# Batch 4's loads issued one chunk earlier, and the order of the first two chunks, in a linear-attention and GELU-MLP kernel

## The chip, the cores and the metric

The kernel runs on one core of a Trainium2 chip. The metric is the device time of one execution in microseconds (us), as the median of several runs. Engines are named as in the profile: PE multiplies matrices, DVE and ACT evict and cast and compute exponentials and GELU, POOL does some elementwise work, and SP issues nearly all DMAs.

## What is computed

Two parts, one after the other. Eight batches of eight heads, 576 positions and 64 channels; then a two-layer MLP over the 4608 resulting rows of 512 channels.

```
q_s = softmax(q, axis=-1)          # over a head's 64 channels
k_s = softmax(k, axis=2)           # over the 576 positions
kv  = einsum('bhsd,bhse->bhde', k_s, v)
att = einsum('bhsd,bhde->bhse', q_s, kv)
x   = att.transpose(0, 2, 1, 3).reshape(4608, 512)
h   = x @ w_in                     # w_in  512 x 2048
out = gelu(h) @ w_out              # exact GELU, w_out 2048 x 512
```

Inputs and output are float32. The kernel multiplies in bfloat16.

## The kernel before

**Chunks.** The rows of the MLP are worked on in nine chunks of 512. Chunk c, for c from 0 to 7, is the first 512 positions of batch c; chunk 8 gathers the last 64 positions of all eight batches. A chunk has two phases. `h_phase` makes h transposed, 16 column tiles t of 128x512, each from four matmuls over the row blocks `dm` of w_in (L295), and applies GELU on ACT into the tile g (L300). `y_phase` makes the output, four tiles j, each from 16 matmuls over t (L305); `y_out` evicts a tile with DVE into one of four `y_sb` buffers (L312) and writes it with a DMA on SP (L315).

**What a chunk needs from attention.** Batch b's q is exponentiated on ACT (`exp_q`, L133), its row sums are made on DVE and it is scaled on POOL or DVE (`norm_q`, L196 to L198). It is transposed to `qT`, for batches 0 and 1 on PE (`tp_mm`, L212, evicted by `tp_evac`) and after that by a DMA transpose on SP (`xbar_step`, L231). k is exponentiated (`exp_k`, L138). v is cast to bfloat16 beside a column of ones (`cast_v`, L145). `kv_mm` (L166) multiplies the two, heads in two halves, `kv_norm` (L176, L177) divides by the sums and gives `kvc`. `x_mm` (L251) multiplies qT by kvc, and `x_evac` (L275 on DVE, L277 on ACT) leaves the chunk's x transposed in `xT`.

**Order.** The schedule is written by hand: every engine executes its instructions in the order in which the program states them. `ins` and `yi` hang pieces of later batches' attention behind chosen matmuls: the entry `(j, t)` runs behind the matmul of output tile j and row t. From chunk 2 on, batch c+2 is loaded in the h phase of chunk c, exponentiated before the y phase of c, and its v is cast behind (0, 8) of that y phase; batch c+1's `x_all` stands behind (2, 12). Chunks 0 and 1 are written out, since w_in and w_out arrive during them.

**DMAs.** SP's queue takes loads, DMA transposes and output writes in program order, and a DMA on it waits for what frees its buffer. Loads of q, k and v use two buffers each (`f32in`), so batch 4 takes batch 2's. Weights arrive in float32 in five staging buffers and are cast to bfloat16 by `cast_wi` (L375 on POOL, L379 on DVE) and `cast_wo` (L398). w_in comes in five column groups; group 2 (columns of t=4 to 7) in four parts by dm, groups 3 and 4 in two parts each, cast in as many pieces as they are loaded. w_out comes in four groups of four rows t; the last one, t=12 to 15, in two halves.

**PSUM.** Eight banks: `psum_h` has three one-bank tiles, `psum_y` two, and `psum_a` one single bank ("a") and one pair ("a2"). h tiles rotate through `psum_h`, output tiles through `psum_y`. In chunk 0 all four output tiles are open at once (`yps`, two in `psum_h` and two in `psum_y`) and t is the outer loop, so that w_out can be used as it arrives.

**The order around the change, before.** After row t=11 of chunk 0's outputs, batch 1's two transposes follow, half 0 in "a" and half 1 in `psum_h`; then rows 12 and 13; the first half of batch 1's kv; rows 14 and 15 for tiles 0 and 1 (`y_end`); the first half of x; the second half of kv; rows 14 and 15 for tiles 2 and 3; the second half of x. Batch 4 is loaded in `front3`, which stands behind t=0 of chunk 2's h phase and first normalises q of batch 3 and transposes it:

```
    def front3():
        norm_q(3, 0, 2)
        norm_q(3, 1, 2, nc.vector)
        xbar_step(3)
        load(4)
```

Of the kernel before, what the change touches and what calls it, by code (L numbers as in the profile page):

```python
# [8 lines left out]
FP32 = mybir.dt.float32  # L9
# [7 lines left out]
def kernel(  # L17
# [74 lines left out]
    def load_pair(b, name, t, parts=1):  # L92
        f = f32in.tile([128, HP, NS * D], FP32, tag=name + "f")
        st[b][name + "f"] = f
        src = t[b].rearrange("h (p n) d -> (h p) (n d)", n=NS).rearrange("(x q) f -> q x f", q=128)
        n = HP // parts
        for i in range(parts):
            nc.sync.dma_start(out=f[:, i * n:(i + 1) * n, :], in_=src[:, i * n:(i + 1) * n, :])

    def load(b):  # L100
        load_main(b, "q", q)
        load_pair(b, "k", k)
        load_pair(b, "v", v)
# [40 lines left out]
    def cast_v(b, hp, eng=nc.vector):  # L144
        eng.tensor_copy(  # L145
            out=v_aug[b % 2][:, hp, :, 0:D],
            in_=st[b]["vf"][:, hp, :].rearrange("p (n d) -> p n d", n=NS),
        )
# [5 lines left out]
    def kv_mm(b, half):  # L154


        if "kv" not in st[b]:
            st[b]["kv"] = psum_a.tile([128, 2, 2, 256], FP32, tag="a2", name="kv")
        ps = st[b]["kv"]
        for n in range(NS):  # L160
            for i in range(2):
                for hh in range(2):
                    hp = 2 * half + i
                    pr = slice(hh * 64, hh * 64 + 64)
                    c = slice((hh ^ i) * 64, (hh ^ i) * 64 + 64)
                    nc.tensor.matmul(  # L166
                        ps[c, i, half, 0:D + 1], ek[b % 2][pr, hp, n, :],
                        v_aug[b % 2][pr, hp, n, 0:D + 1], start=(n == 0), stop=(n == NS - 1),
                    )

    def kv_norm(b, h0, h1):

        ps = st[b]["kv"]
        m = h1 - h0
        rec = small.tile([128, 2, 2], FP32, tag="reck")
        nc.vector.reciprocal(rec[:, :, 0:m], ps[:, :, h0:h1, D])  # L176
        nc.vector.tensor_tensor(  # L177
            out=kvc[b].rearrange("p (h i) d -> p i h d", i=2)[:, :, h0:h1],
            in0=ps[:, :, h0:h1, 0:D],
            in1=rec[:, :, 0:m].unsqueeze(3).to_broadcast([128, 2, m, D]), op=ALU.mult,  # L180
        )
# [21 lines left out]
    def tp_mm(b, half):  # L203
        if half == 0:
            st[b]["qT"] = attn_sb.tile([128, J, HP, 128], BF16, tag="qT", name="qT")
        pool, tag = (psum_h, "h") if half == 1 else (psum_a, "a")
        ps = pool.tile([128, J, 2, 128], BF16, tag=tag)
        st[b][f"tp{half}"] = ps
        for i in range(2):
            hp = 2 * half + i  # L210
            for j in range(J):
                nc.tensor.transpose(  # L212
                    ps[:, j, i, :],
                    st[b]["eq"][:, j, 2 * hp:2 * hp + 2, :].rearrange("p h d -> p (h d)"),
                    identity,
                )
# [19 lines left out]
    def x_tile(b, hp, pool, tag):  # L236
        if "xT" not in st[b]:
            st[b]["xT"] = attn_sb.tile([128, HP, M], BF16, tag="xT", name="xT")
        st[b][f"x{hp}"] = pool.tile([128, M], FP32, tag=tag, name="ps")
# [32 lines left out]
    def x_evac(b, hp, eng="v"):  # L272
        ps = st[b][f"x{hp}"]
        if eng == "v":
            nc.vector.tensor_copy(out=st[b]["xT"][:, hp, :], in_=ps)  # L275
        else:
            nc.scalar.copy(out=st[b]["xT"][:, hp, :], in_=ps)  # L277

    def h_phase(c, ins, groups={}, pre={}):


        g = moe_sb.tile([128, NDF, M], BF16, tag="g", bufs=1)
        st[c]["g"] = g
        xT = st[c]["xT"]
        t1 = 0
        while t1 < NDF:
            t0, t1 = t1, t1 + groups.get(t1, 1)
            ts = range(t0, t1)
            pss = [psum_h.tile([128, M], FP32, tag="h", name="ps") for t in ts]
            for dm in range(NDM):  # L290
                if t0 == 0:
                    for f in pre.get(dm, []):
                        f()
                for ps, t in zip(pss, ts):
                    nc.tensor.matmul(  # L295
                        ps, wi_bf[:, dm, t * 128:(t + 1) * 128], xT[:, dm, :],
                        start=(dm == 0), stop=(dm == NDM - 1),
                    )
            for ps, t in zip(pss, ts):
                nc.scalar.activation(out=g[:, t, :], in_=ps, func=AF.Gelu)  # L300
                for f in ins.get(t, []):
                    f()

    def y_mm(c, ps, j, t):
        nc.tensor.matmul(  # L305
            ps, st[c]["g"][:, t, j * 128:(j + 1) * 128], wo_bf[:, t, :],
            start=(t == 0), stop=(t == NDF - 1),
        )

    def y_out(c, ps, j):  # L310
        y_sb = moe_sb.tile([128, DM], FP32, tag="y_sb")
        nc.vector.tensor_copy(out=y_sb, in_=ps)  # L312
        if c < B:
            dst = out[c * S:c * S + M, :].rearrange("(p j) n -> p j n", j=J)[:, j, :]
            nc.sync.dma_start(out=dst, in_=y_sb)  # L315
        else:
            for b2 in range(2):
                r0 = (2 * j + b2) * S + M
                nc.sync.dma_start(out=out[r0:r0 + R, :], in_=y_sb[b2 * R:(b2 + 1) * R, :])
# [48 lines left out]
    def cast_wi(i, w, eng):  # L368
        n = wi_cols[i]
        r = n // 128  # L370
        o = wi_bf[:, :, wi_off[i]:wi_off[i] + n].rearrange("p d (c m) -> p d c m", c=r)
        w = w[:, :, 0:n].rearrange("p d (m c) -> p d c m", c=r)
        if eng == "p":
            for h in range(2):
                nc.gpsimd.tensor_copy(out=o[:, 2 * h:2 * h + 2], in_=w[:, 2 * h:2 * h + 2])  # L375
        else:
            d = NDM // wi_parts[i]
            for c in range(0, NDM, d):
                nc.vector.tensor_copy(out=o[:, c:c + d], in_=w[:, c:c + d])  # L379

    def load_wo(i, parts=1):
        w = wst.tile([128, 4, DM], FP32, tag="w")
        src = moe_w_out[i * 512:(i + 1) * 512, :]
        if i == 0:
            for h in range(2):
                nc.sync.dma_start(
                    out=w[:, 2 * h:2 * h + 2],
                    in_=src[256 * h:256 * h + 256].rearrange("(p c) f -> p c f", c=2),
                )
            return w  # L390
        src = src.rearrange("(p c) f -> p c f", c=4)
        n = 4 // parts
        for h in range(parts):
            nc.sync.dma_start(out=w[:, h * n:(h + 1) * n], in_=src[:, h * n:(h + 1) * n])
        return w

    def cast_wo(i, w, c0=0, n=4):
        nc.vector.tensor_copy(  # L398
            out=wo_bf[:, 4 * i + c0:4 * i + c0 + n, :], in_=w[:, c0:c0 + n]
        )  # L400

    def warm(n, z=zeros):
        ps = psum_y.tile([128, DM], FP32, tag="y")
# [26 lines left out]
    wo = [load_wo(i) for i in range(3)]  # L430
    load_main(1, "q", q, 2)
    load_pair(1, "k", k, 2)
    wo.append(load_wo(3, 2))
    load_pair(1, "v", v, 4)
    load(2)
    nc.vector.memset(zeros32, 0.0)  # L436
    nc.vector.memset(zeros, 0.0)
# [20 lines left out]
    for hp, pool, tag in ((0, psum_y, "y"), (1, psum_y, "y"), (2, psum_a, "a"), (3, psum_h, "h")):  # L458
# [16 lines left out]
        6: [lambda: cast_wi(4, wi[4], "v")],  # L475
        9: [lambda: cast_wo(0, wo[0])],
        12: [lambda: cast_wo(1, wo[1])],
    }, groups={0: 2})


    exp_q(1, parts=2)
# [5 lines left out]
    norm_q(1, 0, 2)  # L487
    norm_q(1, 1, 2, nc.vector)
    cast_wo(3, wo[3], 0, 2)
    cast_wo(3, wo[3], 2, 2)  # L490
    for hp in range(3):
        cast_v(1, hp, nc.gpsimd)
    for t in range(12):
        for j in range(J):
            y_mm(0, yps[j], j, t)
    tp_step(1, 0)
    tp_step(1, 1)
    cast_v(1, 3)
    load(3)
    for t in (12, 13):  # L500
        for j in range(J):
            y_mm(0, yps[j], j, t)

    def y_end(j):
        for t in (14, 15):
            y_mm(0, yps[j], j, t)

    kv_mm(1, 0)
    kv_norm(1, 0, 1)
    y_end(0)  # L510
    y_end(1)
    y_out(0, yps[0], 0)
    x_tile(1, 0, psum_a, "a")
    x_tile(1, 1, psum_h, "h")
    x_mm(1, 0)
    kv_mm(1, 1)
    x_evac(1, 0, "s")
    x_evac(1, 1, "s")
    kv_norm(1, 1, 2)
    y_out(0, yps[1], 1)  # L520
    y_end(2)
    y_end(3)
    xx = psum_a.tile([128, 2, M], FP32, tag="a2", name="xx")
    st[1]["x2"], st[1]["x3"] = xx[:, 0], xx[:, 1]
    x_mm(1, 1)
    x_evac(1, 2)
    x_evac(1, 3, "s")
    y_out(0, yps[2], 2)
    y_out(0, yps[3], 3)
    h_phase(1, {12: [lambda: cast_v_all(2)]}, groups={0: 2})  # L530
# [9 lines left out]
        (1, 1): [lambda: norm_q(2, 1, 2, nc.vector)],  # L540
        (1, 12): [lambda: kv_step(2)],
        (1, 15): [lambda: xbar_step(2)],
        (2, 2): [lambda: cast_v_all(3)],
        (3, 5): [lambda: x_all(2), lambda: kv_step(3)],
    })

# [2 lines left out]
    def front3():  # L549
        norm_q(3, 0, 2)  # L550
        norm_q(3, 1, 2, nc.vector)
        xbar_step(3)
        load(4)

    for c in range(2, B + 1):
        nb = c + 2
# [54 lines left out]
```

The softmax here doesn't subtract the row's maximum and nothing guards it: scores larger than these inputs give would overflow.

## Time and profile before

| | |
|---|---|
| median of 8 runs | 284.03 us (283.29 to 284.47) |
| the profiled execution | 284.47 us |
| its span in the trace | 282.7 us; 1.8 us lie around it |
| granted PE clock | 1.00 |
| PE, ACT, DVE, POOL busy | 95%, 55%, 36%, 12% of the span |
| DMA | 50.10 MB, mean 177 GB/s |

The span is the time from the first to the last instruction of the program in the trace. Times in the timeline and the chain of waits count from its start. A matmul's shown duration (mean 379 ns for the large ones) overlaps the next one's, so spacing is read from starts. An engine's idle time counts only where PE waits for that engine.

### The profile page before, as it was taken

How to read it: one execution, taken by the hardware profiler on the slowest of the kernel's cores; microseconds unless marked ns; L12 is line 12 of the kernel's file. 1: busy time of each engine (PE TensorE's matmuls, PEld its weight loads, DVE VectorE, ACT ScalarE, POOL GpSimd, SP SyncE). 2: the span in 40 equal slices, each digit the busy share in tenths (PEclk: the TensorE clock that was granted, in tenths of full speed). 3: DMA queues.
4: the chain of work that ended last, by engine and by line, in shares of the span. 5: the costliest groups of instructions: out<-in, count | busy, mean ns of one | idle time of the engine just before them, and what ended most of it. 6: DMA issues, size and time to landing. Idle time of an engine off the chain costs nothing.

```text
span 282.7 us, 4527 instructions
## 1 busy us (share of the span) xinstructions
PE 269.8 (95%) x1894; PEld 125.6 (44%) x1922; DVE 102.2 (36%) x150; ACT 156.7 (55%) x242; POOL 32.8 (12%) x25
## 2 busy tenths in 40 slices
PE   7789999999999899999999999999999999999993
PEld 3334454444444344444444444444444444444442
DVE  3767486309760570075006510552016200220021
ACT  5756763789467915693469436853683363136300
POOL 0530041002020050005000500050005000000000
PEclk9999999999999999999999999999999999999999
DMA  7999999951439429911991189127501500210033
GB/s 243 394 381 430 399 400 406 403 217 57 135 84 347 162 97 242 368 41 39 234 378 50 47 206 358 67 77 178 121 0 74 148 2 0 77 74 0 0 77 75
DMA packets 44852, 50.10 MB, mean 177 GB/s; under 512 B 20384, under 2 KB 29856, under 8 KB 44576
## 3 DMA queue, kind: packets, MB, share of 16 engines
q1 hardware_dynamic: 44544, 49.68, 51.6%
q8 instruction: 15, 0.25, 0.4%
q10 hardware_dynamic: 288, 0.13, 0.2%
q14 instruction: 5, 0.04, 0.0%
HBM read 36.70 MB, written 9.44 MB: 163 GB/s over the span
## 4 chain that ended last, share of the span: by engine, by line
PE 72%; DMA 18%; DVE 4%; ACT 2%; issue 1%; SPq 1%; ACTq 0%
PE ps L295 34%; PE ps L305 33%; DMA f<-in_v_dram 9%; DMA f<-in_q_dram 4%; DMA w<-in_moe_w_in_dram 3%; PE kv L166 2%; DMA touch<-in_moe_w_in_dram 2%; PE ps L251 1%; PE ps L327 1%; DVE v_aug L145 1%; DVE qsum L196 1%; ACT ek L138 1%; ACT e L133 1%; DVE e L198 1%; SPq L231 0%
## 5 line engine op out<-in xcount | busy, mean ns | idle before, releaser
L295 PE MATMUL ps<-xT,wi_bf 128*128 128x512 bf16 x565 | 125.7, 379 | 1.6 <-DVE wi_bf L379 1.0
L305 PE MATMUL ps<-wo_bf,g 128*128 128x512 bf16 x543 | 122.3, 379 | 2.7 <-issue 1.1
L300 ACT ACTIVATE g<-ps 128x512 bf16<-128x512 f32 x144 | 85.6, 597 | 68.7 <-PE ps L295 68.7
L295 PEld LDWEIGHTS <-wi_bf 128*128 128x128 bf16 x576 | 56.1, 98 | 69.6 <-DVE wi_bf L379 1.8
L305 PEld LDWEIGHTS <-g 128*128 128x128 bf16 x560 | 53.9, 98 | 65.5 <-issue 1.8
L312 DVE COPY y_sb<-ps 128x512 f32<-128x512 f32 x35 | 23.8, 683 | 75.3 <-PE ps L305 72.3
L198 POOL TENSOR_TENSOR e<-e,recq 128x2048 bf16<-128x2048 bf16 (+1 forms) x9 | 25.7, 2855 | 179.0 <-DVE recq L197 147.0
L145 DVE CAST v_aug<-f 128x576 bf16<-128x576 f32 x26 | 17.9, 745 | 57.1 <-DMA f<-in_v_dram 57.1
L277 ACT CAST xT<-ps 128x512 bf16<-128x512 f32 x19 | 10.2, 588 | 31.6 <-PE ps L251 22.0
L196 DVE TENSOR_REDUCE qsum<-e 128x16 f32<-128x1024 bf16 (+1 forms) x13 | 21.0, 1614 | 14.5 <-ACT e L133 14.5
L133 ACT ACTIVATE e<-f 128x512 bf16<-128x512 f32 (+1 forms) x42 | 20.5, 556 | 2.0 <-DMA f<-in_q_dram 1.7
L138 ACT ACTIVATE ek<-f 128x2304 bf16<-128x2304 f32 (+1 forms) x10 | 17.2, 1730 | 1.7 <-DMA f<-in_k_dram 1.7
L275 DVE CAST xT<-ps 128x512 bf16<-128x512 f32 x15 | 9.7, 685 | 15.4 <-PE ps L251 12.6
L79 ACT ACT_TABLE_LOAD x9 | 11.5, 1283 | 2.8 <-issue 2.6
L405 PE MATMUL ps<-zeros 128*128 128x512 f32 (+1 forms) x14 | 8.0, 716 | 1.5 <-DVE zeros L436 1.5
L133 ACT ACT_TABLE_LOAD x7 | 9.0, 1283 | 0.1
L379 DVE CAST wi_bf<-w 128x512 bf16<-128x512 f32 (+1 forms) x8 | 7.3, 914 | 2.8 <-DMA w<-in_moe_w_in_dram 2.8
L166 PEld LDWEIGHTS <-ek 64*64 64x64 bf16 x576 | 6.5, 105 | 2.9 <-issue 1.1
L166 PE MATMUL kv<-v_aug,ek 64*64 64x65 bf16 x576 | 7.2, 193 | 0.1
L398 DVE CAST wo_bf<-w 128x2048 bf16<-128x2048 f32 (+1 forms) x5 | 5.1, 1014 | 4.8 <-DMA w<-in_moe_w_out_dram 4.8
L198 DVE TENSOR_TENSOR e<-e,recq 128x1024 bf16<-128x1024 bf16 x4 | 6.4, 1606 | 0.1
L251 PE MATMUL ps<-qT,kvc 64*64 64x512 bf16 x60 | 5.0, 390 | 1.3 <-DVE kvc L177 1.3
(33 smaller groups left out, 41.4 us busy)
## 6 DMA issues: line engine op xcount, KB each, us to landing
out_dram<-y_sb SPq DMA_DIRECT2D x32, 256.0 KB, 2.3
f<-in_k_dram SPq DMA_DIRECT2D x6, 1152.0 KB, 9.6
f<-in_v_dram SPq DMA_DIRECT2D x6, 1152.0 KB, 11.6
f<-in_q_dram SPq DMA_DIRECT2D x6, 1024.0 KB, 7.2
w<-in_moe_w_in_dram SPq DMA_DIRECT2D x6, 512.0 KB, 9.1
f<-in_k_dram SPq DMA_DIRECT2D x4, 576.0 KB, 10.0
f<-in_v_dram SPq DMA_DIRECT2D x8, 288.0 KB, 8.1
f<-in_q_dram SPq DMA_DIRECT2D x4, 512.0 KB, 8.5
```

The lines of the kernel that those rows point to most:

```text
L79: nc.scalar.activation(out=scr[:, 1:2], in_=scr[:, 0:1], func=func)
L133: nc.scalar.activation(out=dst[:, i], in_=src[:, u], func=AF.Exp)
L138: nc.scalar.activation(out=ek[b % 2][:, i:i + n], in_=st[b]["kf"][:, i:i + n].rearrange("p x (n d) -> p x n d", n=NS), func=AF.Exp,)
L145: eng.tensor_copy(out=v_aug[b % 2][:, hp, :, 0:D], in_=st[b]["vf"][:, hp, :].rearrange("p (n d) -> p n d", n=NS),)
L166: nc.tensor.matmul(ps[c, i, half, 0:D + 1], ek[b % 2][pr, hp, n, :], v_aug[b % 2][pr, hp, n, 0:D + 1], start=(n == 0), stop=(n == NS - 1),)
L196: nc.vector.reduce_sum(out=qsum, in_=eq[:, :, hs, :], axis=AX.X)
L198: eng.tensor_tensor(out=eq[:, :, hs, :], in0=eq[:, :, hs, :], in1=recq.unsqueeze(3).to_broadcast([128, J, w, D]), op=ALU.mult,)
L277: nc.scalar.copy(out=st[b]["xT"][:, hp, :], in_=ps)
L295: nc.tensor.matmul(ps, wi_bf[:, dm, t * 128:(t + 1) * 128], xT[:, dm, :], start=(dm == 0), stop=(dm == NDM - 1),)
L300: nc.scalar.activation(out=g[:, t, :], in_=ps, func=AF.Gelu)
L305: nc.tensor.matmul(ps, st[c]["g"][:, t, j * 128:(j + 1) * 128], wo_bf[:, t, :], start=(t == 0), stop=(t == NDF - 1),)
L312: nc.vector.tensor_copy(out=y_sb, in_=ps)
```

## The change

It has two parts. First, `load(4)` moves from `front3` to behind row 2 of output tile 2 of chunk 1, right after the casts of batch 3's v.

Second, chunks 0 and 1 are ordered differently:

- In chunk 0's h phase the tiles t=4 to 7 form one group with dm outside and t inside, as t=0 and 1 did already; t=6 and t=8 take `psum_y` banks. Groups 3 and 4 of w_in are cast in four pieces each; their loads stay in two.
- The load of w_out's last group is cut: rows 12 and 13 stay where they were, rows 14 and 15 come one by one behind batch 1's v. DVE casts the first two, ACT the others.
- Batch 1's transposes share one "a2" pair. Its kv is made in one go after row 13, and its x in one go after row 15 of tiles 0 and 1; row 15 of tiles 2 and 3 comes after that. DVE evicts both x tiles of the second half (ACT had one of them), after output tiles 0 and 1.

The count of large matmuls and the bytes moved stay the same. The unused `pre` argument is dropped.

```
     def tp_mm(b, half):
...
-        pool, tag = (psum_h, "h") if half == 1 else (psum_a, "a")
-        ps = pool.tile([128, J, 2, 128], BF16, tag=tag)
+        if b == 1:
+            if half == 0:
+                st[b]["tp"] = psum_a.tile([128, 2, J, 2, 128], BF16, tag="a2", name="tp")
+            ps = st[b]["tp"][:, half]
+        else:
+            pool, tag = (psum_h, "h") if half == 1 else (psum_a, "a")
+            ps = pool.tile([128, J, 2, 128], BF16, tag=tag)
...
-    def h_phase(c, ins, groups={}, pre={}):
+    def h_phase(c, ins, groups={}, ybanks=()):
...
-            pss = [psum_h.tile([128, M], FP32, tag="h", name="ps") for t in ts]
+            pss = []
+            for t in ts:
+                pool, tag = (psum_y, "y") if t in ybanks else (psum_h, "h")
+                pss.append(pool.tile([128, M], FP32, tag=tag, name="ps"))
...
-            d = NDM // wi_parts[i]
-            for c in range(0, NDM, d):
-                nc.vector.tensor_copy(out=o[:, c:c + d], in_=w[:, c:c + d])
+            for c in range(NDM):
+                nc.vector.tensor_copy(out=o[:, c], in_=w[:, c])
...
+        if i == 3:
+            nc.sync.dma_start(out=w[:, 0:2], in_=src[:, 0:2])
+            return w
...
+    def load_wo_end(w):
+        src = moe_w_out[3 * 512:4 * 512, :].rearrange("(p c) f -> p c f", c=4)
+        for c in (2, 3):
+            nc.sync.dma_start(out=w[:, c], in_=src[:, c])
+
+    def cast_wo(i, w, c0=0, n=4, eng="v"):
+        o, w = wo_bf[:, 4 * i + c0:4 * i + c0 + n, :], w[:, c0:c0 + n]
+        if eng == "v":
+            nc.vector.tensor_copy(out=o, in_=w)
+        else:
+            nc.scalar.copy(out=o, in_=w)
...
-    wo.append(load_wo(3, 2))
+    wo.append(load_wo(3))
     load_pair(1, "v", v, 4)
+    load_wo_end(wo[3])
     load(2)
...
-    }, groups={0: 2})
+    }, groups={0: 2, 4: 4}, ybanks=(6, 8))
...
     cast_wo(3, wo[3], 0, 2)
-    cast_wo(3, wo[3], 2, 2)
...
+    def y_part(t, js):
+        for j in js:
+            y_mm(0, yps[j], j, t)
+
     for t in range(12):
-        for j in range(J):
-            y_mm(0, yps[j], j, t)
+        y_part(t, range(J))
     tp_step(1, 0)
     tp_step(1, 1)
     cast_v(1, 3)
     load(3)
...
-    kv_mm(1, 0)
-    kv_norm(1, 0, 1)
-    y_end(0)
-    y_end(1)
+    cast_wo(3, wo[3], 2, 1, "s")
+    y_part(12, range(J))
+    y_part(13, range(J))
+    kv_step(1)
+    cast_wo(3, wo[3], 3, 1, "s")
+    y_part(14, range(J))
+    y_part(15, (0, 1))
     y_out(0, yps[0], 0)
+    y_out(0, yps[1], 1)
     x_tile(1, 0, psum_a, "a")
     x_tile(1, 1, psum_h, "h")
+    xx = psum_a.tile([128, 2, M], FP32, tag="a2", name="xx")
+    st[1]["x2"], st[1]["x3"] = xx[:, 0], xx[:, 1]
     x_mm(1, 0)
-    kv_mm(1, 1)
+    x_mm(1, 1)
     x_evac(1, 0, "s")
     x_evac(1, 1, "s")
-    kv_norm(1, 1, 2)
-    y_out(0, yps[1], 1)
-    y_end(2)
-    y_end(3)
...
-    x_mm(1, 1)
     x_evac(1, 2)
-    x_evac(1, 3, "s")
+    x_evac(1, 3)
+    y_part(15, (2, 3))
     y_out(0, yps[2], 2)
     y_out(0, yps[3], 3)
...
-        (2, 2): [lambda: cast_v_all(3)],
+        (2, 2): [lambda: cast_v_all(3), lambda: load(4)],
...
     def front3():
         norm_q(3, 0, 2)
         norm_q(3, 1, 2, nc.vector)
         xbar_step(3)
-        load(4)
```

## The prediction

> **What bounds the kernel now.** I read the page first, then the waits of PE, then the chain of waits in order of time, and then the timeline around each wait that these name.
>
> ```profile
> span 282.7 us, 4527 instructions
> PE 269.8 (95%) x1894; PEld 125.6 (44%) x1922; DVE 102.2 (36%) x150; ACT 156.7 (55%) x242; POOL 32.8 (12%) x25
> ```
>
> PE is busy 95% of the span at the full granted clock, so only PE's holes can give time back; work taken from another engine counts only where that engine stands in front of a hole. One 128x512 matmul costs 0.216 us when they follow each other: chunk 2's 64 w_in matmuls start at 76.81 and its w_out matmuls at 90.62, and 13.81 / 64 = 0.216. The waits of PE (engine, line, who ended it, us in total, times, longest) are short enough to show whole:
>
> ```profile
> PE ps L405 <- DVE zeros L436: 1.5, 1, 1.5
> PE ps L251 <- DVE kvc L177: 1.3, 3, 0.6
> PE ps L305 <- issue: 1.1, 7, 0.2
> PE ps L305 <- DVE y_sb L312: 1.1, 1, 1.1
> PE ps L212 <- POOL e L198: 1.1, 1, 1.1
> PE ps L295 <- DVE wi_bf L379: 1.0, 1, 1.0
> ```
>
> L405 and L212 lie before 9.4 us and the diff does not touch them; two of the three kvc waits lie before 14.3. Left are three holes: w_in (L295), kvc in the join of chunks 0 and 1, and y_sb. The timeline (start, us, engine, line, what, and in brackets the idle time before it and who ended it) has them:
>
> ```profile
> 19.41 0.61 DVE L379 CAST wi_bf<-w 128x512 bf16<-128x512 f32 x1 [0.79 <-DMA w<-in_moe_w_in_dram]
> 20.08 9.89 PE L295 MATMUL ps<-xT,wi_bf 128*128 128x512 bf16 x44 [1.01 <-DVE wi_bf L379]
> ...
> 43.48 0.75 DVE L145 CAST v_aug<-f 128x576 bf16<-128x576 f32 x1 [0.91 <-DMA f<-in_v_dram]
> 44.69 0.41 PE L251 MATMUL ps<-qT,kvc 64*64 64x512 bf16 x4 [0.37 <-DVE kvc L177]
> ...
> 95.38 2.73 DVE L145 CAST v_aug<-f 128x576 bf16<-128x576 f32 x4 [13.11 <-DMA f<-in_v_dram]
> 98.02 0.68 DVE L312 COPY y_sb<-ps 128x512 f32<-128x512 f32 x1
> 98.76 2.97 PE L305 MATMUL ps<-wo_bf,g 128*128 128x512 bf16 x13 [1.07 <-DVE y_sb L312]
> ```
>
> The last hole has its cause in the chain of waits:
>
> ```profile
> 82.41 1.32 SPq L231
> ...
> 85.27 10.09 DMA f<-in_v_dram
> 95.35 0.02 issue
> 95.38 2.73 DVE v_aug L145 x4
> 98.11 0.61 DVE y_sb L312
> ```
>
> Batch 4's loads stand in SP's queue behind batch 3's transpose (L231, 82.41). v lands at 95.35, the four v casts then fill DVE to 98.1, and the eviction of chunk 2's first output tile, done computing since about 94.3, is queued behind them; its bank is the one that tile j=2 needs. From 107 us on the chain is PE without a hole, so nothing can be gained there.
>
> **The change part by part.**
>
> *Batch 4's loads.* They now stand behind batch 2's transpose and one output write, so they are issued when chunk 1 is in tile j=2: the transpose starts at 68.94 and takes SP 1.71, the output write 0.5, so q is issued near 71.2, some 12.6 us earlier. The buffers are free: batch 2's exps end at 67.2 and its v casts before 55. From q's issue to v's landing the trace has 95.35 - 83.78 = 11.6 us, so v lands near 82.8. DVE finishes batch 3's normalisation at 82.27 and then casts v at once, 12 us ahead of the first eviction. Tile j=2 starts without a wait at 90.62 + 32 x 0.216 = 97.53 and not at 98.76: **1.23 us**. What the three loads are moved past on SP: output writes of j=2 and j=3 (their data now drain behind 3.3 MB and land up to 6 us later; their y_sb buffers are reused near 94 us or later, so nothing waits) and batch 3's transpose (issued at 82.4, used by the x products at 101.66: 15 us of cover). POOL's queue has none of them. The three DMAs cost SP 1.9 us either way.
>
> *Chunk 0's w_in phase.* Column tiles t=4 to 7 become one group that runs row block by row block, so that 12 matmuls and not 3 can run before the late fourth block; t=6 and t=8 use the idle psum_y banks. Casts of the blocks end at 16.85, 17.99, 18.62 and 20.02. Before, t=4 starts at 18.06, does three matmuls, and waits until 20.08. After: block 0 of t=4, 5, 6 at 18.06, 18.27, 18.49; t=7 needs the bank of t=3, whose GELU ends at 18.86, so it starts at 18.93 (a new wait of 0.22). Blocks 1 to 3 then run from 19.14 to 21.73 without a wait. Next comes t=8, whose blocks are now cast one at a time: both halves of the weights land as before (casts begin at 20.66 and 21.89), four casts end at 21.27, 21.87, 22.51, 23.12, so blocks 2 and 3 of t=8 start at 22.57 and 23.18, and t=9 at 23.40. t=12's blocks are cast by 25.63, before PE is there at 25.99. The w_out phase starts at 23.40 + 7 x 0.864 = 29.44 against 29.80: **0.36 us**.
>
> Here a rule speaks against the split. Row: a 128x512 cast takes 0.61 and a 128x1024 one 1.08, so two halves cost 0.15 more than a whole. The Trainium skill, VectorE: DVE Perf Modes, "The TRN2 errata", says that the fixed cost is paid per instruction, 58 cycles or 0.06 us. By the rule the last cast ends at 23.03 and the part gives 0.45, by the row 0.36. I take the row. (With whole casts block 2 would wait until 23.03, so t=9 would start at 23.46: the split itself gains 0.06.)
>
> *The join of chunks 0 and 1.* Batch 1's v goes ahead of the last two w_out rows (512 KB). In this stretch the 16 DMA engines are full; two 512 KB pieces land at 39.42 and 40.66 (DVE's casts at 39.44 and 40.68 begin with them), so 512 KB are 1.24 us. v's four parts landed at 41.4 to 43.46 and now at 40.15 to 42.2; the two rows at about 42.85 and 43.46. POOL's casts of v end near 42.2, DVE's near 42.97. PE from 39.81 (y's first 48 matmuls): 16 transposes to 40.70 (0.90 before); eight matmuls of rows 12 and 13 to 42.5 (cast by 40.1); kv's first half 0.41 and, after DVE's cast, its second half from 43.03 to 43.5; row 14 to 44.39 (ACT's cast of it ends at 43.45); row 15 for j=0, 1 to 44.9; x products, 0.55, to 45.45 (kvc ready at 44.25); row 15 for j=2, 3 to 45.9. Then the w_in phase of chunk 1 needs x: ACT evicts two tiles to 46.44; DVE evicts y0 and y1 (44.82 to 46.1) and then x's last two tiles, 0.60 apart, the last one to 47.32. So block 3 starts at 47.38 and t=2 at 47.81. The trace has t=2 at 48.59 (w_in matmuls from 46.68, two x evictions late: 14 in 3.58 us). The two parts together: 0.78, the join alone **0.42 us**. The new bound is DVE's row of four evictions; PE alone could be there at 47.63.
>
> The one-bank-pair transpose tile must be evicted (DVE, to 41.8) before kv is written at 42.5: 0.7 us of cover; without it kv would wait. ACT's cast of a 128x512 row from SBUF has no row. Near ones: L277's cast from PSUM, 588 ns, and the exp of that shape, 556 ns. The errata table named above gives ScalarE 224 + 512 cycles, 613 ns. I take 0.59; from 0.56 to 0.61 nothing moves, since row 15 is ready at 44.1 and used at 44.39.
>
> A second rule against: the Trainium skill, DMA: Bandwidth & Descriptors, "Bandwidth", asks for 1 MiB and more per DMA to get 75% of peak; the tail is now two DMAs of 256 KB. At 75% of its 435 GB/s the tail would take 1.6 us (an estimate from that page) and not 1.24: row 15 cast at 44.4, 0.03 lost. v's parts of 288 KB land 0.70 apart, 0.42 MB per us, in the full queue: the row wins. But landings can be uneven: w_in's four 256 KB pieces were cast from 15.76, 17.36, 18.00 and 19.41. A piece 1 us late would cost 0.7, one 0.5 early nothing gained; that is the range of this part: 0.42 from -0.3 to +0.6 (PE alone, and v no longer waited for).
>
> **Sum.** 1.23 + 0.36 + 0.42 = 2.0 us. The profiled execution took 284.47, with a span of 282.7; it becomes 282.5 and 280.7. It was the slowest of the eight shown, 0.44 above their median 284.03. From the median: **282.0**.
>
> **The rivals.**
>
> *The start gives nothing* (late pieces, or the four-bank group waits for GELUs that now come four at a time). For: both depend on landings a few tenths away. Against: 0.3 to 0.8 us of cover at rows 12 to 15. Time: 284.03 - 1.23 = 282.8.
>
> *Batch 4's load gains nothing,* since another wait ends last at 97.5. PE's list has none there and evictions of 0.68 are all DVE has left. Time: 284.03 - 0.78 = 283.25.
>
> *Slower: batch 2's transpose is held up by the loads now right behind it.* It is issued at 68.94, lands 3.7 us later at 72.7, and the x products use it at 73.44: 0.75 us of cover. If its packets shared the DMA engines with 3.3 MB of loads, it could land as late as they do, near 82: a stall of up to 9 us. The kernel is slower by over 0.57 us once the stall exceeds 2.0 + 0.57 = 2.6, that is if the landing takes over 7.0 us. Behind q and k (2.2 MB, some 5.4 us at 405 GB/s) it gives 282.0 + 4.7 = 286.7. Against: batch 4's own transpose at 105.66 has batch 5's loads 2.6 us behind it, at 108.27, and landings are 3.7 to 3.8 us for all seven transposes.
>
> *It does not do what it says:* if the v casts or the loads were still held by a buffer, the three waits would stay: 284.0.
>
> **How the numbers follow.** A measurement of this kernel can tell about 0.2%, 0.57 us, from no change. Both gains 0.72 (281.3 to 282.7), start gives nothing 0.13 (282.5 to 283.4), load gives nothing 0.04, no change 0.05, transpose held up 0.06. The first two and most of the third are faster by over 0.2%: 0.88; same 0.06; slower 0.06. The range 281.3 to 283.2 takes the first case, with 1.1 us at the start as its best end, and most of the second.
>
> **What would show it.** Right: no wait of PE for y_sb; batch 4's loads issued near 70.5 (71.2 less the 0.78 gained by then) and v cast near 82; the w_in wait at 20 us gone, a wait below 0.3 at t=7; the w_out phase of chunk 0 from 29.4; t=2 of chunk 1 at 47.8; chunk 3's w_in phase 2.0 us earlier. Wrong: PE waiting for qT near 72.7, or for wo_bf near 44, or a new wait for y_sb or x in front of chunk 1.

## The result, and the profile after

The changed kernel takes 281.49 us (median of 11 runs, 280.98 to 282.03), against 283.87 for the kernel before on the same chips (32 runs): ratio 0.9915, 95% interval 0.9903 to 0.9927, so 2.4 us less, between 2.1 and 2.8. The forecast was 282.0 in a range of 281.3 to 283.2. The profiled execution took 281.71. Four executions in the rounds below took 579 to 1623 us; medians and ratios leave them out (the 292.2 us quoted in e9's expectation does not).

The page, and the waits of PE (engine, line, who ended the wait, us in total, times, longest). Line numbers have moved by some: L300 is the w_in matmul, L310 the w_out matmul, L317 the eviction, L217 the transpose, L226 its eviction, L256 the x product, L236 the DMA transpose, L383 the cast of w_in.

```profile
span 279.9 us, 4536 instructions
PE 269.6 (96%) x1894; PEld 125.6 (45%) x1922; DVE 102.3 (37%) x152; ACT 156.8 (56%) x243; POOL 32.9 (12%) x25
```

```profile
PE ps L417 <- DVE zeros L449: 1.5, 1, 1.5
PE ps L310 <- issue: 1.1, 7, 0.2
PE ps L256 <- DVE kvc L177: 1.0, 2, 0.6
PE ps L217 <- POOL e L198: 0.9, 1, 0.9
PE tp L217 <- DVE qT L226: 0.8, 1, 0.8
PE kv L166 <- POOL v_aug L145: 0.3, 1, 0.3
```

PE's busy time is what it was (269.6 against 269.8): no work went away, only holes. All three waits that the prediction named (y_sb, wi_bf, and kvc in the join) are gone from this trace. One that it did not name is new: `tp`, 0.8 us. The last line belongs to batch 0, before 12.1 us, where no instruction changed.

The timeline of DVE and of SP's queue in chunks 1 and 2 (start, us, engine, line, what, in brackets the idle time before and who ended it):

```profile
84.72 2.73 DVE L145 CAST v_aug<-f 128x576 bf16<-128x576 f32 x4 [3.00 <-DMA f<-in_v_dram]
93.74 0.69 DVE L317 COPY y_sb<-ps 128x512 f32<-128x512 f32 x1 [6.29 <-PE ps L310]
```

```profile
68.42 1.71 SPq L236 DMA_TRANSPOSE qT<-e  x1
70.23 0.52 SPq L320 DMA_DIRECT2D out_dram<-y_sb  x1
70.80 0.45 SPq L90 DMA_DIRECT2D f<-in_q_dram  x1
...
72.06 0.58 SPq L98 DMA_DIRECT2D f<-in_v_dram  x1
```

The loads are issued at 70.80, 13 us earlier; v is cast at 84.72 and no longer at 95.38; the first eviction of chunk 2 waits for PE alone (93.74, released by L310) and PE runs through. In PE's timeline chunk 2's w_out phase lasts from 90.08 to 105.20, 15.12 us, and lasted 16.34 (90.62 to 106.96):

```profile
90.08 9.88 PE L310 MATMUL ps<-wo_bf,g 128*128 128x512 bf16 x44
99.89 0.63 PE L256 MATMUL ps<-qT,kvc 64*64 64x512 bf16 x8
...
105.20 13.98 PE L300 MATMUL ps<-xT,wi_bf 128*128 128x512 bf16 x63
```

The start of the same timeline, and then that of the kernel before, cut to the lines read here:

```profile
14.93 14.29 PE L300 MATMUL ps<-xT,wi_bf 128*128 128x512 bf16 x62
29.06 10.52 PE L310 MATMUL ps<-wo_bf,g 128*128 128x512 bf16 x47
39.42 0.61 PE L217 MATMUL tp<-identity,e 128*128 128x128 bf16 x8
40.81 0.61 PE L217 MATMUL tp<-identity,e 128*128 128x128 bf16 x8 [0.78 <-DVE qT L226]
41.26 1.89 PE L310 MATMUL ps<-wo_bf,g 128*128 128x512 bf16 x8
...
60.15 6.42 PE L310 MATMUL ps<-wo_bf,g 128*128 128x512 bf16 x28
```

```profile
14.59 4.47 PE L295 MATMUL ps<-xT,wi_bf 128*128 128x512 bf16 x18
...
29.80 10.52 PE L305 MATMUL ps<-wo_bf,g 128*128 128x512 bf16 x47
40.16 1.06 PE L212 MATMUL ps<-identity,e 128*128 128x128 bf16 x16
41.06 1.89 PE L305 MATMUL ps<-wo_bf,g 128*128 128x512 bf16 x8
...
60.68 6.42 PE L305 MATMUL ps<-wo_bf,g 128*128 128x512 bf16 x29
```

The w_in phase of chunk 0 has lost its hole: 14.13 us from its first matmul to the w_out phase's first, against 15.21. The transposes, however, take 1.84 us from the first to rows 12 and 13, against 0.90: the second half waits until DVE has evicted the first.

### The profile page after: what moved, and what is told of

Same layout as the page of the kernel before. It is cut to its first block, busy times and chain, and to the rows that moved or that the text cites. A ratio compares the mean times of both kernels' runs of the same rounds, so it can differ in the third digit from the quotient of the medians.

```text
span 279.9 us, 4536 instructions
## 1 busy us (share of the span) xinstructions
PE 269.6 (96%) x1894; PEld 125.6 (45%) x1922; DVE 102.3 (37%) x152; ACT 156.8 (56%) x243; POOL 32.9 (12%) x25
## 4 chain that ended last, share of the span: by engine, by line
PE 91%; DMA 4%; ACT 2%; issue 1%; DVE 1%; POOL 0%; ACTq 0%
PE ps L300 44%; PE ps L310 41%; DMA f<-in_v_dram 2%; PE kv L166 2%; PE ps L256 2%; DMA f<-in_q_dram 1%; PE ps L332 1%; ACT ek L138 1%; ACT e L133 1%; ACT L133 0%; PE tp L217 0%; DVE qT L226 0%; POOL v_aug L145 0%; PE ps L261 0%; DVE kvc L177 0%
## 5 line engine op out<-in xcount | busy, mean ns | idle before, releaser
L300 PE MATMUL ps<-xT,wi_bf 128*128 128x512 bf16 x566 | 125.6, 379 | 0.6
L310 PE MATMUL ps<-wo_bf,g 128*128 128x512 bf16 x542 | 122.1, 379 | 1.7 <-issue 1.1
L300 PEld LDWEIGHTS <-wi_bf 128*128 128x128 bf16 x576 | 56.1, 98 | 68.6 <-issue 0.7
L310 PEld LDWEIGHTS <-g 128*128 128x128 bf16 x560 | 54.0, 98 | 64.6 <-issue 0.8
L317 DVE COPY y_sb<-ps 128x512 f32<-128x512 f32 x35 | 23.8, 686 | 82.4 <-PE ps L310 79.3
L282 ACT CAST xT<-ps 128x512 bf16<-128x512 f32 x19 | 10.2, 588 | 27.9 <-PE ps L256 18.3
L383 DVE CAST wi_bf<-w 128x512 bf16<-128x512 f32 x12 | 7.3, 657 | 2.2 <-DMA w<-in_moe_w_in_dram 1.9
L256 PE MATMUL ps<-qT,kvc 64*64 64x512 bf16 x60 | 5.0, 390 | 1.0 <-DVE kvc L177 1.0
L410 DVE CAST wo_bf<-w 128x2048 bf16<-128x2048 f32 (+1 forms) x4 | 4.4, 1090 | 3.8 <-DMA w<-in_moe_w_out_dram 3.8
## 6 DMA issues: line engine op xcount, KB each, us to landing
f<-in_v_dram SPq DMA_DIRECT2D x6, 1152.0 KB, 11.6
f<-in_q_dram SPq DMA_DIRECT2D x4, 512.0 KB, 12.5
```

The source lines that it names most:

```text
L256: nc.tensor.matmul(ps[c, :], kvc[b][pr, hp, :], st[b]["qT"][pr, :, hp, :], start=True, stop=True,)
L300: nc.tensor.matmul(ps, wi_bf[:, dm, t * 128:(t + 1) * 128], xT[:, dm, :], start=(dm == 0), stop=(dm == NDM - 1),)
L310: nc.tensor.matmul(ps, st[c]["g"][:, t, j * 128:(j + 1) * 128], wo_bf[:, t, :], start=(t == 0), stop=(t == NDF - 1),)
```

## The experiments

Each edit is against the kernel named; ratios are to the kernel before, with 95% intervals. A table comes first.

| kernel | median us | ratio |
|---|---|---|
| changed | 281.49 | 0.9915 (0.9903 to 0.9927) |
| c1, changed again | 281.69 | 0.9939 (0.9922 to 0.9956) |
| e1, loads alone | 281.74 | 0.9932 (0.9913 to 0.9951) |
| e2, start alone | 283.25 | 0.9994 (0.9980 to 1.0007) |
| e3, group alone | 282.83 | 0.9967 (0.9955 to 0.9980) |
| e4, two transpose tiles | 280.50 | 0.9893 (0.9875 to 0.9910) |
| c2, the same again | 280.84 | 0.9891 (0.9867 to 0.9915) |
| e5, casts later, loads not moved | 281.52 | 0.9932 (0.9912 to 0.9951) |
| e6, loads ahead of the transpose | 291.75 | 1.0296 (1.0268 to 1.0325) |
| e7, e4 with v last | 281.99 | 0.9947 (0.9927 to 0.9966) |
| e8, changed without the group | 281.94 | 0.9928 (0.9902 to 0.9955) |
| c3, before again | 283.86 | 1.0003 (0.9985 to 1.0021) |

**The loads alone (e1).** The kernel before with

```
-        xbar_step(3)
-        load(4)
+        xbar_step(3)
...
-        (2, 2): [lambda: cast_v_all(3)],
+        (2, 2): [lambda: cast_v_all(3), lambda: load(4)],
```

> The kernel before, with load(4) alone moved. Theory (v of batch 4 had held DVE in front of chunk 2's first eviction): PE's wait of 1.07 us for y_sb goes, chunk 2's w_out phase is 1.23 us shorter, 1.2 us faster in all, ratio near 0.9957. Rival (the transpose of batch 2 is held up by the loads behind it): PE waits for qT near 73.4 us, and the kernel is not faster or slower. Rival (gain is in the start alone): no change.

It is 1.9 us faster (0.0068 x 283.67; 1.4 to 2.5), and the wait for y_sb is gone. Its waits of PE:

```profile
PE ps L405 <- DVE zeros L436: 1.5, 1, 1.5
PE ps L212 <- POOL e L198: 1.4, 1, 1.4
PE ps L295 <- DVE wi_bf L379: 1.3, 1, 1.3
PE ps L251 <- DVE kvc L177: 1.0, 2, 0.6
```

No wait for qT came: in its trace the transpose is issued at 68.69 and lands at 72.40, and the x products run at 73.19 without a wait (73.44 in the kernel before). This is most of the whole change.

**The start alone (e2).** The changed kernel with `load(4)` put back behind `xbar_step(3)`.

> The changed kernel with load(4) back in front3: chunks 0 and 1 alone. If the 2.4 us of the whole change are 1.2 from the loads and the rest from the start, this is 1.1 to 1.2 us faster than before (ratio near 0.996) and still has the wait for y_sb near 98 us. By the prediction's sum it is 0.8 us faster. Rival: the start gains next to nothing, as the new wait of 0.8 us of batch 1's second transposes takes it back, and the rest came from the end of the profiled execution; then ratio 0.999 or more.

It is 0.2 us faster, and the interval holds no change: nearer to the rival than to the theory. Its waits of PE show both reasons:

```profile
PE ps L310 <- DVE y_sb L317: 1.3, 1, 1.3
...
PE tp L217 <- DVE qT L226: 0.8, 1, 0.8
```

The new wait of 0.8 us takes back what the group and the rest of the join gain, and the wait for y_sb is 1.3 us here, against 1.1 in the first trace of the kernel before.

**The group alone (e3).** The kernel before with the group of four, `ybanks` and the split casts; the join as before.

> The kernel before with the group of four, the two psum_y banks and the split casts of w_in alone; the join of chunks 0 and 1 as before. Theory (what the first phase saves is worth little as long as v of batch 1 ends the join): chunk 0's w_out phase starts 0.4 to 0.9 us earlier after its w_in phase, but x of chunk 1 waits for kvc as before, since v lands last; 0 to 0.4 us faster. Rival (the saving reaches the end in full): 0.9 us faster, ratio 0.997.

It is 0.9 us faster (0.6 to 1.3). The theory's cap of 0.4 was too low. But how much of that is the group is less plain than the ratio: the hole that it fills is not there in every execution. In the second trace of the kernel before (c3) the four parts of w_in's second group came together, and PE ran through although the group was not there. The timelines of DVE and PE of c3:

```profile
15.71 2.70 DVE L379 CAST wi_bf<-w 128x512 bf16<-128x512 f32 x4 [0.35 <-DMA w<-in_moe_w_in_dram]
```

```profile
14.56 14.23 PE L295 MATMUL ps<-xT,wi_bf 128*128 128x512 bf16 x64
28.63 10.52 PE L305 MATMUL ps<-wo_bf,g 128*128 128x512 bf16 x48
```

Four casts in one piece, and 14.07 us for the phase. In the trace that the prediction was made from, the fourth cast started at 19.41.

**The changed kernel without the group (e8).**

```
-    }, groups={0: 2, 4: 4}, ybanks=(6, 8))
+    }, groups={0: 2})
```

and the casts in `wi_parts` pieces as before.

> The changed kernel without the group of four, the psum_y banks and the split casts of w_in: chunk 0's first phase as before, the join and the moved load as changed. Theory (what the group saves reaches the end, since PE and not a landing now sets the join): 0.9 to 1.2 us slower than the changed kernel, ratio to before near 0.997, with PE's wait for wi_bf back near 19 us. Rival (the join is set by v's landing in any case): ratio 0.9935 as the changed kernel.

At 0.9928 it can't be told from the changed kernel (0.9915 and 0.9939); the interval, 1.5 us wide, also leaves room for a loss of 0.8 us against the mean of these two, so the time does not settle what the group is worth. Its trace does, for one execution: it has the late part, with a wait of PE of 1.28 us, and the phase lasts 15.28 us (14.59 to 29.87). That execution (282.78) was the slowest of e8's six, 0.8 above their median. PE's timeline of it:

```profile
14.59 4.27 PE L300 MATMUL ps<-xT,wi_bf 128*128 128x512 bf16 x19
20.14 9.89 PE L300 MATMUL ps<-xT,wi_bf 128*128 128x512 bf16 x45 [1.28 <-DVE wi_bf L384]
29.87 10.31 PE L310 MATMUL ps<-wo_bf,g 128*128 128x512 bf16 x47
```

The trace of e9 below has the group and a late part as well. DVE's and PE's timelines of e9:

```profile
19.18 0.62 DVE L383 CAST wi_bf<-w 128x512 bf16<-128x512 f32 x1 [1.19 <-DMA w<-in_moe_w_in_dram]
```

```profile
14.72 14.45 PE L300 MATMUL ps<-xT,wi_bf 128*128 128x512 bf16 x64
29.00 10.52 PE L310 MATMUL ps<-wo_bf,g 128*128 128x512 bf16 x48
```

With a late fourth part: 15.2 to 15.3 us without the group (three traces), 14.28 with it. With an early one: 13.83 (e5) and 14.07 without, 14.02 to 14.13 with. So in this phase the group is worth 0.9 to 1.0 us when the part is late, and nothing, or a loss of up to 0.3, when it isn't. The part was late (fourth cast between 19.2 and 19.6, not between 17.8 and 18.3) in 4 of 13 traces: in three of the five without the group and in one of the eight with it, which are too few to tell whether that is chance.

**Two transpose tiles (e4).** The changed kernel with

```
             if half == 0:
-                st[b]["tp"] = psum_a.tile([128, 2, J, 2, 128], BF16, tag="a2", name="tp")
-            ps = st[b]["tp"][:, half]
+                ps = psum_a.tile([128, J, 2, 128], BF16, tag="a", name="tp")
+            else:
+                ps = psum_a.tile([128, 2, J, 2, 128], BF16, tag="a2", name="tp")[:, 0]
```

> The changed kernel, but batch 1's two transpose halves in separate PSUM tiles (half 0 in the single bank, half 1 in the first bank of the pair). Theory (the second half waits for DVE's eviction of the first only because both are in one tile): PE's wait of 0.8 us for qT goes, rows 12 and 13 start 0.8 us earlier; then kv's second half waits for DVE's cast of v, which ends near 42.8, so 0.4 to 0.7 us of it are left at the end, ratio to before near 0.9895. Rival (v's cast or DVE's evictions end last anyway): no gain over the changed kernel, 0.9915.

At 280.50 us it beats both kernels, and it does so again in c2 (280.84).

> The kernel with two transpose tiles (e4_two_tiles) once more: ratio to before near 0.989 to 0.990 again, 1.0 to 1.3 us below the changed kernel, no wait for qT before batch 1's second transposes.

Against the changed kernel it gains about 1.0 us: 0.0035, from 0.9892, the mean of e4 and c2, to 0.9927, the mean of the changed kernel's two ratios. PE's timeline of e4:

```profile
38.80 1.06 PE L218 MATMUL tp<-identity,e 128*128 128x128 bf16 x16
39.69 1.89 PE L311 MATMUL ps<-wo_bf,g 128*128 128x512 bf16 x8
41.51 0.78 PE L166 MATMUL kv<-v_aug,ek 64*64 64x65 bf16 x72
42.22 1.47 PE L311 MATMUL ps<-wo_bf,g 128*128 128x512 bf16 x6
```

All sixteen transposes in one piece, 0.89 us from the first to row 12. By its size each half fills one bank, in both kernels; what differs is that the tile of the changed kernel is one, and its second half waits for the first half's reader.

**v last (e7).** e4 with both halves of the last w_out group ahead of batch 1's v, as before the change.

> The kernel with two transpose tiles (e4_two_tiles), but the last two w_out rows in one DMA ahead of batch 1's v, as before the change. Theory (once PE arrives early, v's landing ends the join): DVE's last cast of v ends 1.2 us later, near 42.6, kv's second half waits 0.6 to 0.7 us for it; 0.5 to 0.7 us slower than with v ahead, ratio near 0.9915. Rival (the order of these loads is hidden anyway): ratio 0.9893 as with v ahead.

It loses 1.5 us of e4's gain (281.99 against 280.50; 0.0054 x 283.6), twice what was expected. PE's timeline of e7:

```profile
41.83 0.81 PE L166 MATMUL kv<-v_aug,ek 64*64 64x65 bf16 x36
42.87 0.22 PE L166 MATMUL kv<-v_aug,ek 64*64 64x65 bf16 x2 [0.23 <-POOL v_aug L145]
43.62 0.47 PE L166 MATMUL kv<-v_aug,ek 64*64 64x65 bf16 x34 [0.54 <-DVE v_aug L145]
44.03 1.47 PE L311 MATMUL ps<-wo_bf,g 128*128 128x512 bf16 x6
```

From kv's first matmul to row 14 it takes 2.20 us where e4 takes 0.71. So the order of the loads is worth 1.5 us once nothing else holds PE back. I had counted DVE's cast alone; POOL's cast of v's third part comes first and is late too.

**The casts later, the loads not moved (e5).** The kernel before with

```
-                yi[(0, 8)] = [lambda nb=nb: cast_v_all(nb)]
+                yi[(1, 12) if c == 2 else (0, 8)] = [lambda nb=nb: cast_v_all(nb)]
```

> The kernel before, with load(4) where it was, and only the four casts of batch 4's v moved from behind (0, 8) to behind (1, 12) of chunk 2's w_out phase, so that DVE meets the first eviction before them. Theory (it is the queueing of the eviction behind the waiting casts that costs, not the late data): PE's wait for y_sb goes and the whole gain of the moved load, 1.2 to 1.9 us, is there without moving the load; ratio 0.993 to 0.996. Rival (late data themselves cost, through kv of batch 4 or the normalisation): a new wait of PE near 100 us, ratio near 1.

It gains what e1 gains, 0.9932, with the loads where they were. DVE's timeline of e5:

```profile
93.60 0.69 DVE L312 COPY y_sb<-ps 128x512 f32<-128x512 f32 x1 [12.01 <-PE ps L305]
...
96.94 2.67 DVE L145 CAST v_aug<-f 128x576 bf16<-128x576 f32 x4
```

The eviction runs 3.3 us ahead of the casts. So the late data cost nothing by themselves; what cost was an eviction queued behind an instruction that waited for them.

**The loads ahead of the transpose (e6, e9).** The changed kernel with `load(4)` six w_out rows earlier (the expectation miscounts three), ahead of `xbar_step(2)` in SP's queue:

```
-        (1, 12): [lambda: kv_step(2)],
+        (1, 12): [lambda: kv_step(2), lambda: load(4)],
```

> The changed kernel with load(4) three w_out rows earlier, behind (1, 12) of chunk 1 and so ahead of batch 2's DMA transpose in SP's queue. It prices the prediction's slower rival. Theory (packets of one queue run in order): the transpose lands behind 3.3 MB, near 80 us and not near 72, and PE waits some 7 us for qT; slower than before by some 5 us, ratio 1.015 to 1.02. Rival (a transpose does not queue behind loads): it lands after 3.7 us, nothing changes, ratio 0.9915.

> The same program as e6_load_first, for its trace (its time was 292.2 us, 8.4 over before). Theory: batch 2's transpose lands 8 to 11 us after the x products ask for it near 72.9 us, behind the moved loads, and PE waits that long there and nowhere else new. Rival: the time goes to output writes or to a later transpose, with waits of PE near 95 us.

It takes 291.8 us, 8.4 more than before (7.6 to 9.2), and 10.1 more than the changed kernel on the same chip (c1). The trace is that of e9, the same program, which took 292.48. SP's queue and PE's wait in it:

```profile
65.97 0.60 SPq L90 DMA_DIRECT2D f<-in_q_dram  x1
...
67.37 0.61 SPq L98 DMA_DIRECT2D f<-in_v_dram  x1
68.34 11.35 SPq L236 DMA_TRANSPOSE qT<-e  x1
```

```profile
PE ps L256 <- DMA qT<-e: 8.9, 1, 8.9
```

The transpose keeps SP for 11.35 us where it took 1.71, until about the time when v lands (12.5 us after its issue, near 79.9). It lands at 81.8, 13.5 us after its issue, and PE waits 8.9 us for it. The rival of the prediction is real, and the order within one queue decides it.

The loss is larger than the wait. The page of e9 gives the granted clock of PE in tenths, in 40 slices of 7.27 us:

```profile
PEclk9999999999759999999999999999999999999999
```

The 7 and the 5 stand for 72.7 to 87.2 us; in the single microseconds from 81 to 86 it is 0.50, from 87 on 1.00 again. From the x products to chunk 2's w_in phase PE takes 5.26 us (81.84 to 87.10), against 3.37 in the changed kernel (72.90 to 76.27), where the clock is 1.00. The wait of 8.9 and these 1.9 make the 10.8 us by which e9 exceeds c1. That PE's long idle time brought the clock down fits this one trace; no run here tests it.

**The two kernels once more (c1, c3).**

> The changed kernel itself once more, on the chip of these runs, as a base for the comparisons: ratio 0.9915 again, PE's wait of 0.8 us for qT in front of batch 1's second transposes again.

> The kernel before once more, for a second trace of it: ratio 1. If its first profile was long in the end (4.1 us from the last eviction to the end of the span against 3.1 in the others), this one has 3.1; PE's wait for y_sb is 1.1 to 1.5 us again.

c1 shows the changed kernel's wait of 0.8 us again; its gain is smaller, 1.7 us (0.0061 x 283.47) and not 2.4, and the two intervals overlap only from 0.9922 to 0.9927. c3's ratio is 1; its wait for y_sb is 1.4 us, and its end is as long as the first trace's, against what was expected.

## Why the prediction was right, point by point

**Batch 4's loads: right, and the main part.** The mechanism is shown twice, by e1, which takes the data's lateness away, and by e5, which takes only the queueing away. The size was near: 1.23 us predicted, 1.22 in the pair of traces. In time e1 and e5 gain 1.9 each, with 1.4 as the lower end. The y_sb hole varies: chunk 2's w_out phase lasted 16.34 us before; in c3 the wait is 1.4 and not 1.1, in e2 1.3. A hole of 1.2 to 1.6 explains most of the 1.9, and the rest is within the interval or in the end of the execution (last section).

**Where v lands: off, without effect.** Predicted near 82.0 with the start's gain; it was 84.7, since q, k and v took 13.9 us from q's issue and not 11.6. The cover of 12 us became one of 9.

**The group in chunk 0: mechanism right, size off.** The step "after" gave 0.36, with t=8 waiting for its split casts. With a late fourth part the phase saves 0.9 to 1.0 (e8 against e9). The term was mis-sized for two reasons. t=8 hardly waited: in the trace of the changed kernel two casts of 128x512 that follow each other start 0.54 apart (20.32 and 20.86) and end at 21.48, so a pair costs 1.16 against 1.08 for one of twice the size; I had taken 1.24 from casts that stood alone, against the Trainium skill's 0.06 us per instruction (VectorE: DVE Perf Modes, "The TRN2 errata"). For casts in a row the page's 0.06 was nearer (0.08 here) than my 0.15; the same section adds that a single op showed some 150 cycles of fixed time, not 58, which the prediction left out. And the hole was taken as fixed, where it comes and goes with the landing of one part.

**The join: the step that failed.** "16 transposes to 40.70 (0.90 before)". They took 1.84. The text named the cover between the pair's eviction and kv, and missed the wait inside the pair, where the second half's transposes wait for DVE's eviction of the first. It cost more than the 0.42 that the part was to bring: from chunk 0's first w_out matmul to chunk 1's the changed kernel takes 31.09 us (29.06 to 60.15), and the kernel before took 30.88 (29.80 to 60.68). e2, which adds the new join to e3's group, gains 0.2 us where e3 gains 0.9 and where 0.78 was predicted for the start. e4, which takes only this wait away, needs 30.14 us for that stretch (28.44 to 58.58) and gains 1.0. In five traces each the old join takes 30.4 to 31.5 us for it and the changed one 31.1 every time. The bound that the prediction named instead, DVE's row of four evictions, hardly held: chunk 1's w_in phase takes 13.87 us in the changed kernel and in e4, against 13.81 in later chunks.

**What stands ahead of v.** That v's place was worth something was right, but in the changed kernel the new wait hides it: kv starts at 43.08, after DVE's cast (42.07 and 0.74). e7 shows its worth, 1.5 us, once the wait is gone.

**ACT's casts and the small pieces.** ACT took 618 ns for a cast of 128x512 from SBUF, against 0.59 taken and 613 from the page. The two rows landed near 41.8 and 42.4, some 0.6 us apart, so 256 KB pieces in a full queue lost nothing against 1.24 for 512 KB (the Trainium skill, DMA: Bandwidth & Descriptors, "Bandwidth", asks for larger ones; here the row held).

**The rivals.** The start giving nothing was nearly so (e2), but for another reason than late pieces. The moved load giving nothing is refuted by e1. The transpose held up does not happen behind its own place in the queue, and costs 8.9 us of wait when it is behind the loads (e9); I had put 4.7 to 9 on it. So the forecast of the whole, 2.0 against 2.4 measured (1.7 in c1), came out of a load term that was somewhat small and a start term that was too large; that the two errors nearly cancel is luck. In the pair of traces the spans differ by 2.8 us: 1.22 from the y_sb hole, 1.08 from chunk 0's w_in phase, and 1.0 from the end of the execution (last section), less 0.21 in the join and 0.34 by which chunk 0 began later. The 1.08 rests on when one part lands, and the 1.0 stood in no term of the prediction.

## What to carry to other kernels

An instruction that waits for a DMA should stand in its engine's order behind every eviction that can be ready before the data; moving the waiter three instructions back (behind an eviction and the two operations after it) was worth as much as moving 3.4 MB of loads. Where DMA transposes and loads share a queue, the transpose that is needed first goes first: the same loads six w_out rows earlier turned a gain of about 2 us into a loss of 8.4. Two halves that one engine writes and another reads in turn belong in two tiles, even if one tile spans both banks.

## What the runs showed of the hardware

A DMA's landing in a full queue is not a fixed time: the fourth 256 KB part of w_in's second group had landed when DVE reached it, between 17.8 and 18.3 us, in nine traces, and kept DVE waiting until 19.2 to 19.6 in four, of programs whose DMAs are alike up to there. One trace of a kernel shows one draw of it.

From the last eviction's end to the end of the span the two traces of the kernel before took 4.10 and 4.11 us, the traces of c1, e1 to e5, e7, e8, c2 and the changed kernel 3.04 to 3.38, though e3 has the same DMAs in the same order as the kernel before. In the two long ones the slowest of the last four output writes landed 3.1 us after its issue, in the others 2.4. Whether this is chance or belongs to the program is open, and it bears on how much of e1's and e5's 1.9 us is the hole alone. e2 speaks against a fixed second of the kernel before: its trace has the wait for y_sb and the short end, and its gain is 0.2 us.

The changed kernel shows e9's effect in small. Batch 3's transpose, issued at 81.87 while batch 4's v was still on its way (cast at 84.72), kept SP for 4.05 us and landed 6.1 us after its issue; in the kernel before it was 1.32 and 3.7. The x products use it at 99.89, so PE did not wait for it: of the 15 us of cover in the prediction some 12 were left.
